# VectorE's scores on ScalarE's free rows, and packed Q and attention outputs, in a two-layer attention and mixer kernel

## The chip, the core and the metric

The kernel runs on one core of one Trainium2 chip. The metric is device time in microseconds. The program is one launch, with all inputs and the output in device memory.

## The reference

Two layers, each an attention block and a mixer block with an MLP, on one sequence of S = 2048 tokens of width D = 512, in bfloat16:

```
def A(x, wq, wk, wv, wo):              # 32 heads of width 16, one shared K and V
    q = heads(x @ wq); k = x @ wk; v = x @ wv
    p = softmax(einsum("bhqd,bkd->bhqk", q, k) * 16 ** -0.5)
    return merge(einsum("bhqk,bkd->bhqd", p, v)) @ wo
def B(x, w1, w2, w3, w4):
    h = gelu(layernorm(x) @ w1)
    hs = shift(h quarters by +1, -1, +2, -2 tokens) @ w2
    x1 = x + hs
    return x1 + gelu(layernorm(x1) @ w3) @ w4     # w3: 512 x 1792
for layer in range(2):
    x = x + A(layernorm(x), ...)
    x = x + B(layernorm(x), ...)
```

The scores are 32 x 2048 x 2048 per layer; their exponentials are most of the elementwise work.

## The kernel before

**The program is written by a planner.** `Plan` (line 32) is a small simulator that runs when the kernel is built. Each `op` has an engine, what it reads and writes, a guessed duration and a priority (a lower number goes first). `run` steps through time, `_pick` chooses for each free engine the ready operation of lowest priority number, `_place` gives it its start. `emit` then writes each engine's instructions in that fixed order, with semaphore waits. On the chip the order does not change. A DMA goes to SP's queue; each has a semaphore of its own.

**Attention.** A layer's queries are cut into chunks (`CHUNKS`, line 450): four of 512 tokens in layer 0; three of 512 and two of 256 in layer 1. Within a chunk, the loops run over 8 blocks `b` of four heads, over 16 key tiles `kb` of 128 tokens, and over two halves `p` of two heads each. A half is a unit: 2 heads x 128 keys x 512 queries (with 256 queries, two key tiles). There are 2048 units. The heads of a block lie in four groups of 32 SBUF rows, of which 16 carry data, so the score matmul of one head (`qk`, line 846) uses 32 of the array's 128 rows, and matmuls of different heads can run at the same time.

A unit goes one of two ways:
- `declare_unit` (line 879): two score matmuls into two PSUM banks (slots 0-1 and 2-3 in turn), one exponential of 128 x 1024 on ScalarE into EA (line 895), and the product with V (line 966), which adds into the bank ACC.
- `declare_pair` (line 901): two score matmuls (line 851) into two banks of the common pool, two VectorE instructions that write the exponent bits as uint16 into J (line 916), two shift adds of 43 and 85 into JK (line 924), and three products with V copies scaled by `PARTS`. So a pair is two L916, two L924 and three times the V product.

`assign` (line 1063) decides which units become pairs. It looks `AHEAD` = 7 halves ahead for one whose half is `ndve % 2`, so pairs take the two halves in turn; at most two pairs are unfinished, and VectorE's backlog must be under 4 us. It is called whenever the planner's time moves on (`pump`, line 1038). A pair's scores have priority 0.5, but `deferred` (line 225) gives them `ALONE` = 11 except where they can join score matmuls that are just running: then, on other rows, they go beside them (riding).

The pool has three PSUM banks (5, 6, 7), shared by pairs and by all side work.

**Side work.** `block_end` (line 974) closes a block: a copy of ACC (L998), sums, reciprocals, a product that spreads them (L1020), and a multiplication into OT (L1026). After a chunk's last block, `chunk_end` (line 1086) declares the output projection (L1124: eight matmuls of 16 used rows in 32 per tile, WO being padded with zeros), the mixer, the MLP, in layer 0 the next layer's layer norm, K and V, and the Q projection of the chunk after next (`qproj`, line 765). The Q projection writes each block with four column groups of 32, so that head h lands on rows 32h (L781, 16 matmuls a block), and one copy (L788). Side work has priority 10, behind the V products (2) and ahead of lone pairs; `URGE` sets a chunk's own number (1.5 for layer 0's last chunk), and `PACE` spreads its PE work. The mixer's Y tiles are a ring of six, so a chunk's mixer waits for the MLP of the tiles that hold its slots.

In layer 1, chunk 0 begins before all keys are there (`EARLY`); its partial sums are copied out (`SPILL`), and the Q of chunk 1 is written as they come free.

**Dummy matmuls.** `filler` (L868) puts a 512-column matmul of zeros on PE when the planner's running account (`KEEP`, `CREDIT`, `CAP`, `URGENT`, `FORCE`) finds that PE has worked too little. Side matmuls of full width are taken in its place where some are ready.

**Engines.** ScalarE has the exponentials and the GELUs, VectorE the pairs, all copies out of PSUM and the layer norms' elementwise work, POOL the roots of the variances and fills, SP the loads and 16 output stores.

Of the kernel before, what the change touches and what calls it, by code (L numbers as in the profile page):

```python
# [26 lines left out]
class Op:  # L27
    __slots__ = ("eng", "emit", "preds", "npend", "succ", "dur", "prio", "seq", "ready", "start",
                 "end", "take", "give", "dma", "out", "pos", "sem", "vc", "side", "placed", "pe", "feeds")


class Plan:
# [7 lines left out]
    DRAIN = {"ACT": 0.15, "DVE": 0.085, "POOL": 0.1}  # L40
    SELF = 0.035
    MARGIN = 0.2
# [5 lines left out]
    CREDIT = 0.3  # L48
    URGENT = 0.4
    FORCE = 0.6  # L50
    CAP = 1.0
    WAITING = 12.0
    BUNCH = 2
    ALONE = 11
    PATIENCE = 3.0
    SLACK = 0
    NEAR_FILL = 0.2

    def __init__(self, nc, pool_banks):
# [14 lines left out]
        self.lane = [0.0] * 4  # L74
        self.window = 0
# [8 lines left out]
        self.units = []  # L84

    def op(self, eng, emit, reads=(), writes=(), dur=0.1, prio=None, take=None, give=None,
           dma=0, out=False, side=True, pe=None):
# [3 lines left out]
        o.pe = pe  # L91
        o.feeds = None
# [184 lines left out]
    def _place(self, o, t):  # L277
# [5 lines left out]
        if o.dma:  # L283
            s = max(t + 1.6, self.dma_free)
            o.end = s + o.dma / 330e3 + 0.6
            self.dma_free = s + o.dma / 330e3
            self.free_at[o.eng] = t + 0.06
# [21 lines left out]
        else:  # L309
            self.free_at[o.eng] = t + o.dur  # L310
            o.end = t + o.dur + self.DRAIN[o.eng]
        heapq.heappush(self.events, self.free_at[o.eng])
        if o.give is not None:
            self.pool.append((o.end, o.give.bank))
            self.pool_last[o.give.bank] = o
            heapq.heappush(self.events, o.end + self.LAT["PE"])
            heapq.heappush(self.events, o.end + self.MARGIN)
        for s in o.succ:
# [42 lines left out]
    def emit(self):  # L361
# [6 lines left out]
        nd = 0  # L368
        for o in todo:
            kn = known[o.eng]  # L370
            cand = []
# [19 lines left out]
            if o.dma:  # L391
                nd += 1
                key = f"d{nd}"
                sems[key] = nc.alloc_semaphore(key)
                o.sem = (key, 16)
# [13 lines left out]
        def body(eng):  # L409
            def f(e):  # L410
                for waits, emit, sem, inc in code[eng]:
                    for k, v in waits:
                        e.wait_ge(sems[k], v)
                    emit(e).then_inc(sem, inc)
# [33 lines left out]
class Kernel:  # L448
# [4 lines left out]
    URGE = ((10, 10, 10, 1.5), (10, 10, 10, 10, 10))  # L453
# [8 lines left out]
    STEPS = (0, 43, 85)  # L462
    PARTS = (0.3203125, 0.25390625, 0.2021484375)
# [3 lines left out]
    AHEAD = 7  # L467
    MAX_PAIRS = 2
    BACKLOG = 4
# [24 lines left out]
    def memory(self):  # L494
# [13 lines left out]
        self.WO = sb("WO", [8, 512])  # L508
# [8 lines left out]
        self.OT = sb("OT", [8, 512])  # L517
# [14 lines left out]
        self.SM = sb("SM", [5, 16], dt.float32)  # L532
# [34 lines left out]
    def build(self):  # L567
        with contextlib.ExitStack() as self.stack:
# [3 lines left out]
            self.pl.filler = self.filler if self.FILL else None  # L572
            self.pl.run(self.pump)
            self.pl.emit()

    def head(self):
# [42 lines left out]
        for j in range(3):  # L619
            fill("POOL", self.VD[:, j, :, :, 16:17], self.PARTS[j], vd, 0.2, -7)  # L620
        for c in range(4):
# [3 lines left out]
            if c == 0:  # L625
                self.qproj(0, 0, prio=-6, blocks=(0,))
            if c == 2:
                self.qproj(0, 0, prio=-5, blocks=range(1, 8))
# [5 lines left out]
        fill("POOL", self.WO, 0.0, [("WO",)], 3.5, 3)  # L634
        fill("POOL", self.GP[:, 0, :, 0:2], 0.0, [("GPL", 0)], 0.1, 3)
        wo4 = ins["A_wo"].rearrange("(b g d) n -> g d b n", b=8, g=4, d=16)
        for g in range(4):
            load(self.WO[32 * g:32 * g + 16, :, :], wo4[g], [("WO",)], 131072, 5)
# [15 lines left out]
    def rstd(self, tiles, prio, both=False):  # L654
# [4 lines left out]
        s0, s1, s2, s3, s4 = (self.SM[:, i, a:b] for i in range(5))  # L659
# [10 lines left out]
        root(s0, mv, s4, tg("MV"), tg("R1"), tg("S4"))  # L670
        if both:
# [4 lines left out]
            root(s3, s2, s4, tg("S2"), tg("R2"), tg("S4"))  # L676

# [24 lines left out]
    def ln_in(self, la, tiles, prio=None):  # L702
# [6 lines left out]
        for tb in tiles:  # L709
            op("DVE", lambda e, tb=tb: e.tensor_scalar(  # L710
                out=self.ZR[:, tb % 4, :], in0=src(tb), scalar1=self.MV[:, tb, 0:1],
                scalar2=self.SM[:, 0, tb:tb + 1], op0=ALU.subtract, op1=ALU.mult),
               reads=[("X", tb), ("MV", tb), ("R1", tb)], writes=[("ZR", tb % 4)], dur=0.456 if la else 0.355, prio=prio)
# [51 lines left out]
    def qproj(self, la, c, prio=None, blocks=range(8)):  # L765
# [7 lines left out]
        for b in blocks:  # L773
# [18 lines left out]
    def make_groups(self):  # L792
# [34 lines left out]
        self.di = 0  # L827
# [10 lines left out]
        self.pairs = []  # L838
# [480 lines left out]
```

## Time and profile before

| | us |
|---|---|
| median of 3 runs (1708.56 to 1714.65) | 1708.66 |
| the profiled execution | 1708.95 |
| its span, first to last instruction | 1707.2 |
| PE busy, matmul | 1672.0 |
| ScalarE busy | 1545.6 |
| VectorE busy | 1398.7 |
| POOL busy | 62.6 |
| mean granted TensorE clock, share | 0.999 |

A row of a group reads: line, engine, operation, output and inputs with their shapes, count | busy time, mean ns of one | idle time of the engine just before them, and what ended it. A row of the waits reads: who waited for whom, us in total, times, longest. Times of stretches count from the span's start. PE's busy time has overlapping matmuls and modelled ends, so a busy PE is not PE at its peak.

### The profile page before, as it was taken

How to read it: one execution, taken by the hardware profiler on the slowest of the kernel's cores; microseconds unless marked ns; L12 is line 12 of the kernel's file. 1: busy time of each engine (PE TensorE's matmuls, PEld its weight loads, DVE VectorE, ACT ScalarE, POOL GpSimd, SP SyncE). 2: the span in 40 equal slices, each digit the busy share in tenths (PEclk: the TensorE clock that was granted, in tenths of full speed). 3: DMA queues.
4: the chain of work that ended last, by engine and by line, in shares of the span. 5: the costliest groups of instructions: out<-in, count | busy, mean ns of one | idle time of the engine just before them, and what ended most of it. 6: DMA issues, size and time to landing. Idle time of an engine off the chain costs nothing.

```text
span 1707.2 us, 37918 instructions
## 1 busy us (share of the span) xinstructions
PE 1672.0 (98%) x16522; PEld 555.0 (33%) x16522; DVE 1398.7 (82%) x2957; ACT 1545.6 (91%) x1632; POOL 62.6 (4%) x129
## 2 busy tenths in 40 slices
PE   8999999999999999999999999999999999999999
PEld 3322223323322222323223432223223224444444
DVE  8887999889998789898677568899889988668752
ACT  3999999999999999998978499999999999998912
POOL 2000000000000000000000000000000000000000
PEclk9999999999999999999999999999999999999999
DMA  5000000000000000000000000000000000000000
GB/s 186 2 1 1 1 1 1 1 1 1 2 2 1 1 1 1 2 1 1 1 1 1 1 1 2 2 1 2 5 4 4 2 1 2 8 8 2 2 13 16
DMA packets 10199, 12.42 MB, mean 7 GB/s; under 512 B 1584, under 2 KB 9520, under 8 KB 10032
## 3 DMA queue, kind: packets, MB, share of 16 engines
q1 hardware_dynamic: 10032, 10.00, 1.8%
q8 instruction: 129, 2.11, 0.5%
q14 instruction: 38, 0.31, 0.1%
HBM read 7.90 MB, written 2.10 MB: 6 GB/s over the span
## 4 chain that ended last, share of the span: by engine, by line
ACT 52%; PE 43%; DVE 4%; DMA 0%; issue 0%; POOL 0%; SPq 0%; POOLq 0%
ACT EA L895 48%; PE PB L851 14%; PE PB L966 11%; PE PB L1267 4%; PE PB L1236 4%; PE PB L868 3%; ACT G L1253 2%; PE PB L1124 2%; PE PB L1203 1%; PE PB L781 1%; ACT L895 1%; DVE J L916 1%; PE PB L690 1%; PE PB L1159 1%; DVE ST L649 1%; PE PB L1020 1%
## 5 line engine op out<-in xcount | busy, mean ns | idle before, releaser
L895 ACT ACTIVATE EA<-PB 128x1024 bf16<-128x1024 f32 x1558 | 1438.7, 1077 | 93.0 <-PE PB L851 56.6
L916 DVE TENSOR_SCALAR J<-PB 128x512 uint16<-128x512 f32 x980 | 634.4, 684 | 100.5 <-PE PB L851 95.5
L851 PE MATMUL PB<-QT,KT 32*128 32x512 bf16 (+1 forms) x4608 | 661.9, 359 | 14.4 <-ACT EA L895 9.9
L966 PE MATMUL PB<-EA,VP 128*32 128x512 bf16 (+1 forms) x3510 | 416.6, 360 | 1.0 <-DVE ACCF L994 0.3
L924 DVE TENSOR_SCALAR JK<-J 128x1024 uint16<-128x1024 uint16 x980 | 363.4, 420 | 37.7 <-PE PB L966 35.5
L851 PEld LDWEIGHTS PB<-QT,KT 32*128 32x128 bf16 x4608 | 172.2, 91 | 553.9 <-ACT EA L895 431.1
L966 PE MATMUL PB<-JK,VD 128*32 128x512 bf16 (+1 forms) x2196 | 256.9, 361 | 0.3 <-DVE JK L924 0.3
L966 PE MATMUL PB<-J,VD 128*32 128x512 bf16 (+1 forms) x1098 | 158.9, 362 | 0.4 <-DVE J L916 0.2
L966 PEld LDWEIGHTS PB<-EA,VP 128*32 128x32 bf16 x3510 | 111.7, 94 | 129.6 <-issue 107.2
L868 PE MATMUL PB<-ONES,NIL 128*128 128x512 bf16 x421 | 135.8, 394 | 11.5 <-DVE ST L649 2.5
L1236 PE MATMUL PB<-ZT,W 128*128 128x384 bf16 (+2 forms) x560 | 125.4, 339 | 0.4 <-DVE X L1130 0.3
L1267 PE MATMUL PB<-W,G 128*128 128x512 bf16 x448 | 121.4, 382 | 1.7 <-ACT G L1253 1.5
L966 PEld LDWEIGHTS PB<-JK,VD 128*32 128x32 bf16 x2196 | 71.4, 95 | 91.2 <-issue 47.9
L1246 DVE CAST G<-PB 128x512 bf16<-128x512 f32 (+2 forms) x126 | 73.2, 583 | 21.1 <-PE PB L1236 18.7
L781 PE MATMUL PB<-YT,WQ 128*32 128x512 bf16 (+1 forms) x1152 | 77.0, 359 | 0.1
L1124 PE MATMUL PB<-WO,OT 128*128 128x512 bf16 x256 | 74.1, 383 | 0.0
L868 PEld LDWEIGHTS PB<-ONES,NIL 128*128 128x128 bf16 x421 | 36.1, 98 | 86.6 <-issue 23.3
L1253 ACT ACTIVATE G<-G 128x3584 bf16<-128x3584 bf16 (+2 forms) x18 | 46.0, 2601 | 18.2 <-DVE G L1246 18.1
L666 POOL TENSOR_SCALAR SM<-MV 128x4 f32<-128x4 f32 (+3 forms) x30 | 8.9, 295 | 1363.7 <-DVE MV L651 1363.7
L1236 PEld LDWEIGHTS PB<-ZT,W 128*128 128x128 bf16 x560 | 41.4, 97 | 48.9 <-issue 26.3
L1026 DVE TENSOR_TENSOR OT<-ACCF,PB 128x512 bf16<-128x512 bf16 (+1 forms) x72 | 44.7, 622 | 11.6 <-PE PB L1020 11.2
L966 PEld LDWEIGHTS PB<-J,VD 128*32 128x32 bf16 x1098 | 43.2, 94 | 30.3 <-issue 22.2
(83 smaller groups left out, 850.2 us busy)
## 6 DMA issues: line engine op xcount, KB each, us to landing
W<-in_B_w_dram SPq DMA_DIRECT2D x2, 1792.0 KB, 12.3
X<-in_A_x_dram SPq DMA_DIRECT2D x8, 256.0 KB, 6.4
out_dram<-OUTB SPq DMA_DIRECT2D x16, 128.0 KB, 1.7
W<-in_B_w_dram SPq DMA_DIRECT2D x2, 512.0 KB, 6.5
WQ<-in_A_wq_dram SPq DMA_DIRECT2D x1, 512.0 KB, 5.8
WO<-in_A_wo_dram SPq DMA_DIRECT2D x4, 128.0 KB, 3.2
WK<-in_A_wk_dram SPq DMA_DIRECT2D x1, 16.0 KB, 6.0
WV<-in_A_wv_dram SPq DMA_DIRECT2D x1, 16.0 KB, 6.0
```

Source lines behind the costliest of these rows:

```text
L781: ins = e.matmul(self.PB[32 * g:32 * g + 32, L.bank, 0:n], lhsT=self.WQ[:, dc, w0:w0 + 32], rhs=self.YT[:, slot, dc, n0:n0 + n], start=(dc ...
L851: ins = e.matmul(self.PB[:, bank, j * n:(j + 1) * n], lhsT=self.KT[32 * h:32 * h + 32, la, (kb + j) * 128:(kb + j + 1) * 128], rhs=self.QT ...
L868: "PE", lambda e: e.matmul(self.PB[:, self.ACC if L is None else L.bank, :], lhsT=self.NIL, rhs=self.ONES, start=L is not None, stop=L is ...
L895: o = q.feeds = op("ACT", lambda e: e.activation(self.EA[:, ea, :, :], self.PB[:, b0:b0 + 2, :], ACTF.Exp, scale=0.25), writes=bk + [("EA" ...
L916: o = op("DVE", lambda e, i=i, L=L: e.tensor_scalar(out=J[:, i * 512:(i + 1) * 512], in0=self.PB[:, L.bank, :], scalar1=128 * LOG2E * 0.25 ...
L924: o = op("DVE", lambda e, k=k, r=r: e.tensor_scalar(out=self.JK[:, r, :], in0=J, scalar1=float(self.STEPS[k]), scalar2=None, op0=ALU.add), ...
L966: ins = e.matmul(self.PB[32 * h:32 * h + 32, self.ACC, 0:w], lhsT=v[:, la, kb + j, :], rhs=ap[:, i, j * w:(j + 1) * w], start=first and j ...
L1124: ins = e.matmul(self.PB[:, L.bank, :], lhsT=self.OT[:, b, q:q + 128], rhs=self.WO[:, b, :], start=(b == 0), stop=(b == 7))
L1236: ins = e.matmul(self.PB[:, L.bank, 0:n], lhsT=self.W3[:, dc, f * 128:(f + 1) * 128], rhs=ZT[:, dc, 0:n], start=(dc == 0), stop=(dc == 3))
L1246: op("DVE", lambda e, f=f, L=L: e.tensor_copy(self.G2[:, f, 0:n], self.PB[:, L.bank, 0:n]), writes=[L, ("G2", f)], dur=t_ps(n), give=L)
L1253: ins = e.activation(self.G2[:, a:a + 7, 0:n], self.G2[:, a:a + 7, 0:n], ACTF.Gelu_apprx_tanh)
L1267: ins = e.matmul(self.PB[:, L.bank, :], lhsT=self.G2[:, f, i * 128:(i + 1) * 128], rhs=self.W4[:, f, :], start=(f == 0), stop=False)
```

## The change

**Riding by rule.** When the planner places a score matmul of a ScalarE unit, it now calls `attach`: if two pool banks are free, a pair of the other half is declared at once. `assign` takes the half as an argument, looks between 2 and 22 halves ahead, and is otherwise called only when no pair was declared for 4 us.

```
+        if o.feeds is not None and self.attach is not None:
+            self.attach(o)
...
-        if self.assign(now):
+        if now > self.attached + self.LONELY and self.assign(now, self.ndve % 2):
...
+    def attach(self, q):
+        if sum(1 for t, b in self.pl.pool if t + 0.06 <= self.pl.now) >= self.FREE:
+            self.assign(self.pl.now, 1 - q.pe[3][0] // 2)
...
-        d = max(self.di, self.hi + self.AHEAD)
-        while d < len(self.halves) and (self.halves[d][7] or self.halves[d][5] != self.ndve % 2):
+        d = self.hi + self.AHEAD
+        while d < len(self.halves) and (self.halves[d][7] or self.halves[d][5] != p or d in self.given):
             d += 1
-        if d >= len(self.halves):
+        if d >= min(len(self.halves), self.hi + self.AHEAD + self.FAR):
             return False
```

**Constants.**

```
-    URGE = ((10, 10, 10, 1.5), (10, 10, 10, 10, 10))
+    URGE = ((10, 10, 10, 1.0), (10, 10, 10, 1.5, 10))
-    AHEAD = 7
+    AHEAD = 2
-    BACKLOG = 4
+    BACKLOG = 6
+    FAR = 20
+    FREE = 2
+    LONELY = 4
-    MARGIN = 0.2
+    MARGIN = 0.15
-    CREDIT = 0.3
-    URGENT = 0.4
+    CREDIT = 0.2
+    URGENT = 0.6
-    CAP = 1.0
-    WAITING = 12.0
+    CAP = 0.5
+    WAITING = 16.0
-    ALONE = 11
+    ALONE = 8
-    SLACK = 0
+    SLACK = 0.05
```

**Q packed.** Except for blocks 0 and 1 of the first chunk and all of layer 1's chunk 1 (`direct`), Q is projected two blocks at a time with all 128 columns (4 matmuls for each two blocks), copied to QS, and moved to the rows 32h of QT by two operations of four DMAs each. QT is cleared once by POOL.

```
+        for k in () if direct else range(blocks[0] // 2, blocks[-1] // 2 + 1):
...
+                        ins = e.matmul(self.PB[:, L.bank, 0:n], lhsT=self.WQ[:, dc, 128 * k:128 * k + 128],
+                                       rhs=self.YT[:, slot, dc, n0:n0 + n], start=(dc == 0), stop=(dc == 3))
...
+            op("DVE", lambda e, k=k, L=L: e.tensor_copy(self.QS[:, k, 0:n], self.PB[:, L.bank, 0:n]),
...
+            for j in range(2):
+                op("SP", lambda e, j=j: [
+                    e.dma_start(self.QT[32 * h:32 * h + 16, par, 2 * k0 + j:2 * k1:2, 0:n],
+                                self.QS[64 * j + 16 * h:64 * j + 16 * h + 16, k0:k1, 0:n]) for h in range(4)],
```

**Attention outputs packed.** L1026 writes OS (two slots) in place of OT, and four DMAs move the 16 used rows of each head into an OT of four full tiles. WO is no longer padded (one load in place of four and a clearing), and the output projection takes 4 matmuls per tile.

```
+        op("SP", lambda e: [
+            e.dma_start(self.OT[r0 + 16 * h:r0 + 16 * h + 16, b // 2, 0:n], self.OS[32 * h:32 * h + 16, m, 0:n])
+            for h in range(4)], reads=[("OS", m)], writes=[("OT", b)], dma=128 * n, parts=4, prio=5)
...
-        for h in range(4):
+        for h in range(2):
...
-                                   start=(b == 0), stop=(b == 7))
+                                   start=(b == 0), stop=(b == 3))
```

An operation of the planner may now hold several DMAs (`parts`); the DMAs use 80 semaphores in turn, each waiting for the last use of its own.

**Shift adds.** A constant second operation is added; the code can put adds and layer-norm products on POOL, but `ADDS = 0` and `LN_ENG = "DVE"` keep them on VectorE.

```
-            o = op("DVE", lambda e, k=k, r=r: e.tensor_scalar(
-                out=self.JK[:, r, :], in0=J, scalar1=float(self.STEPS[k]), scalar2=None, op0=ALU.add),
+            x = op(eng, lambda e, k=k, r=r: e.tensor_scalar(
+                out=self.JK[:, r, :], in0=J, scalar1=float(self.STEPS[k]), scalar2=1.0, op0=ALU.add,
+                op1=ALU.mult),
```

The same second operation (`scalar2=0.0, op1=ALU.add`) stands in the product L1143.

149 lines of the change are left out of this document (101 added, 48 removed).

## The prediction

> **What bounds the kernel now.** I read the busy time by stage first (columns: stretch, its length, busy time and instructions of PE, PEld, DVE, ACT and POOL, granted clock, DMA share, GB/s), then the costliest groups, then the waits of each stage.
>
> ```profile
> 50.00:750.00 700.00, 694.89 (x6606) 206.47 (x6600) 620.16 (x1299) 695.91 (x741) 17.61 (x36) 1.00 0.01 1
> 750.00:1000.00 250.00, 239.03 (x1846) 80.39 (x1844) 176.77 (x372) 200.03 (x202) 10.45 (x20) 1.00 0.00 1
> 1000.00:1450.00 450.00, 446.63 (x4645) 138.21 (x4642) 394.55 (x822) 448.47 (x480) 9.18 (x19) 1.00 0.01 2
> 1450.00:1620.00 170.00, 165.39 (x2454) 71.24 (x2453) 130.09 (x289) 158.94 (x165) 7.85 (x16) 1.00 0.02 5
> 1620.00:1707.00 87.00, 81.23 (x450) 39.80 (x448) 35.37 (x75) 19.99 (x25) 4.98 (x14) 1.00 0.04 14
> ...
> 450.00:500.00 50.00, 49.61 (x492) 15.21 (x494) 47.91 (x99) 49.93 (x53) 0.19 (x1) 1.00 0.01 1
> ```
>
> In three stages (50 to 750, 1000 to 1450, 1450 to 1620) ScalarE is full or nearly so: 1303.3 of 1320 us. In the fourth, around the change of layer (750 to 1000), it is idle for 50 us, and in the tail the work is a chain with little in parallel. PE looks full everywhere, but that counts dummy matmuls and overlapping ends. VectorE is idle for 79.8 + 55.5 + 39.9 = 175.2 us in the three stages where ScalarE is the limit. So time can come from two places: units moved from ScalarE to VectorE, and an earlier end of the side work that stands alone at 750 to 1000 and after 1620.
>
> ```profile
> L895 ACT ACTIVATE EA<-PB 128x1024 bf16<-128x1024 f32 x1558 | 1438.7, 1077 | 93.0 <-PE PB L851 56.6 <-PE PB L966 35.4
> L916 DVE TENSOR_SCALAR J<-PB 128x512 uint16<-128x512 f32 x980 | 634.4, 684 | 100.5 <-PE PB L851 95.5
> L924 DVE TENSOR_SCALAR JK<-J 128x1024 uint16<-128x1024 uint16 x980 | 363.4, 420 | 37.7 <-PE PB L966 35.5
> ...
> L868 PE MATMUL PB<-ONES,NIL 128*128 128x512 bf16 x421 | 135.8, 394 | 11.5 <-DVE ST L649 2.5 <-DVE MV L651 1.7 <-DVE ZR L1222 1.6
> L781 PE MATMUL PB<-YT,WQ 128*32 128x512 bf16 (+1 forms) x1152 | 77.0, 359 | 0.1
> L1124 PE MATMUL PB<-WO,OT 128*128 128x512 bf16 x256 | 74.1, 383 | 0.0
> ```
>
> There are 2048 units: 1558 exponentials on ScalarE at 1438.7/1558 = 0.923 us, and 490 pairs on VectorE (two L916, two L924 each) at (634.4 + 363.4)/490 = 2.036 us.
>
> **Riding.** The price of a pair's scores that do not ride stands in two bursts of L851 of four matmuls each, two for a ScalarE unit and two for a pair: where both use the same two heads they take 0.60 us, where they use different ones 0.39.
>
> ```profile
> 122.50 0.60 PE L851 MATMUL PB<-QT,KT 32*128 32x512 bf16 x4
> 126.05 0.39 PE L851 MATMUL PB<-QT,KT 32*128 32x512 bf16 x4
> ...
> 126.52 1.29 DVE L916 TENSOR_SCALAR J<-PB 128x512 uint16<-128x512 f32 x2 [1.21 <-PE PB L851]
> 127.72 1.42 DVE L924 TENSOR_SCALAR JK<-J 128x1024 uint16<-128x1024 uint16 x4
> 129.23 1.29 DVE L916 TENSOR_SCALAR J<-PB 128x512 uint16<-128x512 f32 x2
> ```
>
> Today the pair's heads alternate by count, so riding is luck; what does not ride waits at priority 11, behind all side work. The change declares a pair when a ScalarE unit is placed, for the other two heads, if two banks are free, and lowers the lone priority to 8. What that can give back is the time VectorE waits for L851 (first row of each stage; the second is the wait of L924 for a buffer that L966 still reads):
>
> ```profile
> DVE J L916 <- PE PB L851: 40.7, 57, 4.0
> DVE JK L924 <- PE PB L966: 15.4, 19, 2.0
> ...
> DVE J L916 <- PE PB L851: 18.3, 37, 1.6
> DVE JK L924 <- PE PB L966: 9.3, 21, 1.3
> ...
> DVE J L916 <- PE PB L851: 14.7, 16, 6.1
> DVE JK L924 <- PE PB L966: 5.9, 7, 1.6
> ```
>
> That is 73.7 us in the three stages. I take three quarters, 55 us; nothing of the 30.6 us on L966, since more pairs bring more of those matmuls.
>
> **Repacked Q.** Q blocks of 16 used rows in 32 become full 128-row products. Directly written stay 2 blocks of the first chunk and the 8 of layer 1's chunk 1; the rest become 3 + 5 x 4 copies of 512 columns and 8 of 256. So of 72 copies 31 go: 23 long ones and 8 short ones.
>
> ```profile
> L788 DVE CAST QT<-PB 128x512 bf16<-128x512 f32 x56 | 37.7, 684 | 5.0 <-PE PB L781 4.8
> L788 DVE CAST QT<-PB 128x256 bf16<-128x256 f32 x16 | 6.5, 413 | 1.1 <-PE PB L781 1.0
> ```
>
> 23 x 37.7/56 + 8 x 6.5/16 = 18.7 us of VectorE. With the 55 us that is 74 us. A pair moved costs VectorE 2.036 us and shortens the stage by 0.923, in which VectorE would also have worked, so 74/(2.036 + 0.923) = 25 pairs, and ScalarE's stages end 25 x 0.923 = **23 us earlier**. The planner's other constants (margins, credits, how far ahead a pair may lie) change only the order that it writes; no row prices them, and I leave them inside these bounds. With no wait gone, 18.7/2.96 = 6 pairs, 6 us; with VectorE as full as at 450 to 500 (47.91 of 50, so 55 us of idle left in 1320), (175 - 55 + 18.7)/2.96 = 47 pairs, 43 us. A loss is a rival below.
>
> **The shift add** gets a second operation (multiply by one). No row shows a constant second one. Two rows differ by an operation and a pointer:
>
> ```profile
> L1143 DVE TENSOR_SCALAR ZR<-Y,SM 128x512 bf16<-128x512 bf16 x32 | 10.5, 343 | 0.1
> L710 DVE TENSOR_SCALAR ZR<-X,MV,SM 128x512 bf16<-128x512 bf16 x16 | 5.8, 405 | 0.0
> ```
>
> At worst 62 ns on each of 980 adds, 61 us, 61/2.96 = 21 pairs, 19 us. I take zero: L916 already does two operations, and the pointer is the likelier owner of the 62 ns; the end stays in the range. The ZR product L1143 gets the same second operation, at worst 2 us in all. The POOL paths of the adds and layer norms are switched off and cost nothing.
>
> **PE slots and the tail.** A 512-column slot costs 3.02/14 = 0.216 us:
>
> ```profile
> 1632.59 3.02 PE PB L1267 x14
> ```
>
> Four 32-column L781 matmuls share a slot, so 72 blocks are 288 slots; after, 10 x 4 + 31 x 4 = 164. The 124 saved (92 long, 32 half as long) are 23 us. L1124 goes from 256 to 128 matmuls, 128 x 0.216 = 28 us. Of these 51 us, the layer-1 part ahead of the tail is chunk 2's Q (16 slots), chunks 3 and 4 (32 half slots) and 14 tiles of L1124 (56 slots): 104 - 16 = 88 slots, 19 us. In the tail the chain stands so:
>
> ```profile
> 1617.29 2.85 ACT L895 ACTIVATE EA<-PB 128x1024 bf16<-128x1024 f32 x3 [0.55 <-PE PB L966]
> 1624.43 6.27 ACT L1253 ACTIVATE G<-G 128x3584 bf16<-128x3584 bf16 x2 [2.99 <-DVE G L1246]
> 1635.87 0.69 DVE L1278 TENSOR_TENSOR OUTB<-PB,X 128x512 bf16<-128x512 f32 x1 [3.94 <-PE PB L1263]
> 1636.48 0.54 DVE L1139 TENSOR_SCALAR Y<-X,MV,SM 128x512 bf16<-128x512 f32 x1
> ```
>
> After the last exponential (1620.1) the MLP of chunk 2 is still to get its GELU, and chunk 3's mixer starts only at 1636.5, when that MLP has freed the ring of six Y tiles. Side work is last in priority, so 19 us of PE freed ahead of it pull this MLP forward, and chunk 3's own work now has urgency 1.5. I take 13 of the 19, since 170 us with PE at 165.4 also hold dummies that free slots may only replace. Chunk 4's chain gets new links: four DMAs after the last block, then 8 matmuls where 16 stood.
>
> ```profile
> L1282 SPq DMA_DIRECT2D out_dram<-OUTB x16: 332/332/372, 1230.4 to 1705.0; - x16
> out_dram<-OUTB SPq DMA_DIRECT2D x16, 128.0 KB, 1.7
> WK<-in_A_wk_dram SPq DMA_DIRECT2D x1, 16.0 KB, 6.0
> ```
>
> No copy inside the chip stands in the trace. Four issues and a landing lie between 4 x 0.33 + 1.7 = 3.0 us and 1.3 + 6.0 = 7.3; I take 3.0, because the 6.0 was taken behind the input loads, less 8 x 0.216 = 1.7 saved: +1. Tail: **-12 us**, bounds -30 (most of chunk 2's 26 us gone) and +6.
>
> SP's queue gets 64 Q issues and 288 for the outputs, 3 less for WO: 349 x 0.33 = 116 us over the span. SP has nothing but 16 output stores after the loads, which come behind them in the queue. A DMA that waits for VectorE holds those behind it; Q is double-buffered by chunk, so that costs nothing unless it is the last output of a chunk.
>
> **Change of layer and head.** The 50 us that ScalarE is idle at 750 to 1000 are a chain of GELUs, layer norms and W4 products. 16 of its slots go (3.5 us), urgency rises from 1.5 to 1.0, and a DMA wait of 3.0 us (which the next chunk's units can cover) comes in. I take **-5**, bounds -15 and +8. In the head, 12 slots (2.6 us) and three copies (2.0) go: **-2**, bounds -4 and +2; the new clearing of QT takes about the place in which POOL clears WO today.
>
> The sum: -23 - 12 - 5 - 2 = -42. The profiled execution took 1708.95 us (span 1707.2), against a median of 1708.66, so no correction: **1667 us**.
>
> **Rivals.** *VectorE is its own limit.* The waits for L851 close, but the time goes to waits for L966 and for side work's banks, and the freed slots are filled with dummies. Then 6 us from the copies and some 5 from tail and head remain: 1698. For it: POOL and banks are unchanged, and L924's 30.6 us are there already. Against: at 126 to 130 L916, L924 and L916 follow each other with no gap once scores are early. The Trainium skill, "TensorEngine Tiling (Array Packing)", section PSUM Bottleneck, says that packing speeds up TensorE but not the emptying of PSUM, which may become the bound; by that alone this rival would hold. The trace agrees in part: the pair above needs 1.29 us to empty what PE wrote in 0.39.
>
> *Fewer pairs (slower).* A pair needs two of three banks free at the moment a unit's scores are placed; where side work holds two, the fallback gives one pair per 4 us. L916 ran 488 times in 50 to 750, a pair per 2.87 us:
>
> ```profile
> 50.00:750.00 700.00, 315.24 (x488) 1.00 0.01 1
> ```
>
> If half of the 1320 us fell to one per 4 us, 660 x (1/2.87 - 1/4) = 65 pairs went back to ScalarE, +60 us, less 19 of the other terms: 1750. It decides once more than 19/0.923 = 21 pairs are lost. For it: side work is in most stretches. Against: a pair's banks are empty 1.29 us after its scores, and units come every 0.92.
>
> *The clock.* In the head, a stretch with PE busy 1.71 of 3.4 us was followed by one at a granted 0.53, with 8 matmuls in 3.11 us.
>
> ```profile
> 5.40:8.80 3.40, 1.71 (x7) 1.00 1.02 334
> 8.80:12.20 3.40, 3.11 (x8) 0.53 1.10 309
> ```
>
> Such a stretch loses 3.11 - 8 x 0.216 = 1.4 us of PE. With 51 us of dense work out and dummies rarer (cap 0.5, urgent 0.6), 40 of them would cost 56 us of PE, of which I let half reach the end: 1667 + 28 = 1695. Against: every stage after the head was granted 1.00. [...]
>
> *More.* VectorE as full as at 450 to 500 and chunk 2's MLP out of the tail: 1708.95 - 43 - 30 - 5 - 2 = 1629.
>
> *Not done.* If the planner finds no free banks at all, every pair comes from the fallback, which is the slower rival at its end and counted in it.
>
> **How the numbers follow.** Forecast 0.56, VectorE its own limit 0.15, fewer pairs 0.12, clock 0.05, more 0.12. The forecast's own range is 1640 to 1700. For 8 in 10 the range runs from 1624 (just past "more") to 1712 (past the limit and clock rivals, and 1667 with the add's 19 us and the upper ends of tail and change of layer, 18 + 13, which is 1717, all but reached); fewer pairs and a remainder are left out. A measurement tells about 0.5%, 8.5 us: faster is under 1700.1, slower over 1717.2. Faster: 0.54 + 0.12 + 0.07 of the limit and clock rivals = 0.73; slower: most of fewer pairs and the add's worst end, 0.12; same 0.15.
>
> **What would show it.** Right: some 1030 L916 and 1533 exponentials; VectorE's wait for L851 under 25 us in the three stages; bursts of four at 0.39 us; 284 Q and 128 output matmuls; the add still at 420 ns; 75 us from last exponential to end; SP issues landing within about 2 us. Wrong: fewer than 980 L916, an add of 480 ns, stages with a clock under 1.00, dummies well above 421, or a tail still of 87 us.

## The result, and the profile after

The changed kernel takes **1650.28 us** (median of 4 runs, 1650.17 to 1650.58), beside 1709.0 for the kernel before (4 runs, 1708.56 to 1714.65): a ratio of 0.9649, 95% interval 0.9629 to 0.967. The forecast was 1667, with a range of 1624 to 1712. The profiled execution has a span of 1648.8 us, 58.4 less than before.

Lines have moved: the exponential is now L961, the scores L917, the V product L1039, the exponent bits L982, the shift add L992, the dummies L934. The first view is the busy time by stage (columns as in the prediction):

```profile
50.00:750.00 700.00, 681.48 (x6193) 206.16 (x6271) 626.31 (x1307) 698.09 (x743) 18.28 (x36) 1.00 0.04 7
750.00:1000.00 250.00, 238.01 (x2049) 81.17 (x2078) 204.20 (x442) 219.04 (x224) 11.06 (x20) 1.00 0.01 3
1000.00:1450.00 450.00, 438.07 (x4404) 140.14 (x4442) 398.53 (x828) 445.42 (x471) 13.67 (x25) 1.00 0.04 9
1450.00:1620.00 170.00, 162.73 (x2156) 74.20 (x2174) 134.09 (x295) 140.84 (x143) 8.61 (x22) 1.00 0.03 9
1620.00:1648.00 28.00, 24.76 (x130) 11.86 (x131) 6.22 (x15) 6.88 (x14) 1.11 (x2) 1.00 0.04 15
```

ScalarE is as full as before from 50 to 750 and from 1000 to 1450. Around the change of layer it now works 219.04 of 250 us where it worked 200.03, and the granted clock is 1.00 in every stage. The costliest groups, of the kernel after:

```profile
L961 ACT ACTIVATE EA<-PB 128x1024 bf16<-128x1024 f32 x1541 | 1425.2, 1058 | 57.1 <-PE PB L1039 31.5 <-PE PB L917 24.3
L982 DVE TENSOR_SCALAR J<-PB 128x512 uint16<-128x512 f32 x1014 | 656.4, 683 | 103.9 <-PE PB L917 100.0
L992 DVE TENSOR_SCALAR JK<-J 128x1024 uint16<-128x1024 uint16 x1014 | 381.8, 419 | 21.3 <-PE PB L1039 15.7
L934 PEld LDWEIGHTS PB<-ONES,NIL 128*128 128x128 bf16 x340 | 28.7, 98 | 71.8 <-issue 27.9 <-DVE J L982 12.4 <-DVE JK L992 5.2
L828 DVE CAST QS<-PB 128x512 bf16<-128x512 f32 (+1 forms) x31 | 18.7, 609 | 1.5 <-PE PB L824 1.3
```

There are 17 units fewer on ScalarE (1558 to 1541) and 17 pairs more (980 to 1014 L982). The add with two operations costs 419 ns, as with one. Dummies fell from 421 to 340; they are counted by their weight loads here, because some matmul records are missing (276 of 340 are there).

The end of the span, in ScalarE's timeline of the kernel after (start, length, what it did, what it was idle for before):

```profile
1546.92 6.27 ACT L1330 ACTIVATE G<-G 128x3584 bf16<-128x3584 bf16 x2
...
1575.42 1.06 ACT L1253 ACTIVATE GP<-GP 128x1024 bf16<-128x1024 bf16 x1
1586.26 1.02 ACT L961 ACTIVATE EA<-PB 128x1024 bf16<-128x1024 f32 x1 [0.50 <-PE PB L917]
1600.79 3.28 ACT L1330 ACTIVATE G<-G 128x1792 bf16<-128x1792 bf16 x2 [12.21 <-DVE G L1323]
```

In the kernel before, chunk 2's MLP GELU (the 128 x 3584 one) ran at 1624.43, behind the last exponential, and chunk 3's mixer GELU later still:

```profile
1648.23 1.06 ACT L1173 ACTIVATE GP<-GP 128x1024 bf16<-128x1024 bf16 x1 [17.53 <-DVE GP L1169]
```

Now the MLP GELU starts 39 us before the last exponential does, and chunk 3's mixer GELU is ahead of it too. What is left behind the last exponential is chunk 3's MLP and chunk 4.

A span can be added up along ScalarE: its idle time in the first 50 us, its busy time up to the last exponential, its idle time around the change of layer (750 to 1000 us), its other idle time before the last exponential, and the tail behind that. From the two traces, in us:

| | before | after | difference |
|---|---|---|---|
| idle, head | 27.7 | 22.6 | -5.1 |
| busy up to the last exponential | 1525.8 | 1524.7 | -1.1 |
| idle, change of layer | 50.0 | 31.0 | -19.0 |
| other idle | 16.7 | 9.0 | -7.7 |
| tail | 87.0 | 61.5 | -25.5 |
| span | 1707.2 | 1648.8 | -58.4 |

The busy time hides two movements: exponentials fell by 13.5 us (1438.7 to 1425.2), and some 12 us of GELUs and table loads came in: 7 of them stood in the tail before, and four more table loads (34 for 30, 1.28 us each) make 5. Three quarters of the gain (19.0 and 25.5) lie where side work stands alone.

### The profile page after: what moved, and what is told of

It is laid out like the page before. It is cut to its first block, busy times and chain, and to the rows that moved or that the text cites. A ratio compares the mean times of both kernels' runs of the same rounds, so it can differ in the third digit from the quotient of the medians.

```text
span 1648.8 us, 36207 instructions
## 1 busy us (share of the span) xinstructions
PE 1589.5 (96%) x15333; PEld 531.6 (32%) x15521; DVE 1413.3 (86%) x2994; ACT 1537.7 (93%) x1619; POOL 67.9 (4%) x130
## 4 chain that ended last, share of the span: by engine, by line
ACT 60%; PE 35%; DVE 3%; issue 1%; DMA 0%; POOL 0%; SPq 0%; POOLq 0%
ACT EA L961 56%; PE PB L917 11%; PE PB L1039 9%; PE PB L1344 5%; PE PB L1313 3%; ACT G L1330 2%; PE PB L1206 1%; PE PB L1239 1%; ACT L961 1%; PE PB L737 1%; DVE J L982 1%; PE PB L934 1%; PE PB L824 1%; ACT GP L1253 1%; DVE ST L677 1%
## 5 line engine op out<-in xcount | busy, mean ns | idle before, releaser
L961 ACT ACTIVATE EA<-PB 128x1024 bf16<-128x1024 f32 x1541 | 1425.2, 1058 | 57.1 <-PE PB L1039 31.5
L982 DVE TENSOR_SCALAR J<-PB 128x512 uint16<-128x512 f32 x1014 | 656.4, 683 | 103.9 <-PE PB L917 100.0
L917 PE MATMUL PB<-QT,KT 32*128 32x512 bf16 (+1 forms) x4608 | 624.7, 360 | 20.9 <-ACT EA L961 15.4
L1039 PE MATMUL PB<-EA,VP 128*32 128x512 bf16 (+1 forms) x3472 | 450.8, 361 | 1.7 <-DVE ACCF L1067 0.5
L992 DVE TENSOR_SCALAR JK<-J 128x1024 uint16<-128x1024 uint16 x1014 | 381.8, 419 | 21.3 <-PE PB L1039 15.7
L917 PEld LDWEIGHTS PB<-QT,KT 32*128 32x128 bf16 x4608 | 159.1, 91 | 540.8 <-ACT EA L961 462.3
L1039 PE MATMUL PB<-JK,VD 128*32 128x512 bf16 (+1 forms) x2272 | 316.4, 360 | 0.9 <-DVE JK L992 0.7
L1039 PE MATMUL PB<-J,VD 128*32 128x512 bf16 (+1 forms) x1136 | 182.5, 361 | 4.1 <-DVE J L982 4.1
L1039 PEld LDWEIGHTS PB<-EA,VP 128*32 128x32 bf16 x3472 | 118.8, 94 | 142.6 <-issue 122.0
L1039 PEld LDWEIGHTS PB<-JK,VD 128*32 128x32 bf16 x2272 | 88.6, 95 | 98.0 <-issue 49.8
L934 PE MATMUL PB<-ONES,NIL 128*128 128x512 bf16 x276 | 90.2, 395 | 7.9 <-DVE ZR L720 2.2
L1330 ACT ACTIVATE G<-G 128x3584 bf16<-128x3584 bf16 (+2 forms) x18 | 46.0, 2601 | 16.4 <-DVE G L1323 16.3
L1039 PEld LDWEIGHTS PB<-J,VD 128*32 128x32 bf16 x1136 | 49.0, 94 | 37.1 <-issue 23.7
L1099 DVE TENSOR_TENSOR OS<-ACCF,PB 128x512 bf16<-128x512 bf16 (+1 forms) x72 | 44.7, 620 | 10.3 <-PE PB L1093 8.0
L934 PEld LDWEIGHTS PB<-ONES,NIL 128*128 128x128 bf16 x340 | 28.7, 98 | 71.8 <-issue 27.9
L1344 PEld LDWEIGHTS PB<-W,G 128*128 128x128 bf16 x448 | 31.3, 97 | 49.5 <-issue 30.4
L677 DVE BATCH_NORM_STATS2 ST<-X 128x6 f32<-128x512 f32 (+1 forms) x64 | 42.9, 678 | 3.7 <-DMA X<-in_A_x_dram 3.3
```

The lines of the kernel that those rows point to most:

```text
L677: op("DVE", lambda e, tb=tb: e.bn_stats(self.ST6[:, tb, :], src(tb)), reads=[tagf(tb)], writes=[("ST", tb)], dur=0.606, prio=prio)
L917: ins = e.matmul(self.PB[:, bank, j * n:(j + 1) * n], lhsT=self.KT[32 * h:32 * h + 32, la, (kb + j) * 128:(kb + j + 1) * 128], rhs=self.QT ...
L934: "PE", lambda e: e.matmul(self.PB[:, self.ACC if L is None else L.bank, :], lhsT=self.NIL, rhs=self.ONES, start=L is not None, stop=L is ...
L961: o = q.feeds = op("ACT", lambda e: e.activation(self.EA[:, ea, :, :], self.PB[:, b0:b0 + 2, :], ACTF.Exp, scale=0.25), writes=bk + [("EA" ...
L982: o = op("DVE", lambda e, i=i, L=L: e.tensor_scalar(out=J[:, i * 512:(i + 1) * 512], in0=self.PB[:, L.bank, :], scalar1=128 * LOG2E * 0.25 ...
L992: x = op(eng, lambda e, k=k, r=r: e.tensor_scalar(out=self.JK[:, r, :], in0=J, scalar1=float(self.STEPS[k]), scalar2=1.0, op0=ALU.add, op1 ...
```

## The experiments

The prediction's theory: freed PE slots end side work sooner, and VectorE's freed time takes pairs from ScalarE at 0.923 us a unit, so the parts add. The rivals: VectorE is its own limit, so that little but the copies counts; the clock, because dummies are made rarer; and, formed on the result, that no part brings much alone, because a freed slot that the planner fills with a dummy or leaves to work that isn't late is worth little: only the parts together bring the side work of a chunk ahead of the point where ScalarE runs out. Last, that one order of instructions is luckier than another.

The change has three parts, and each experiment takes the kernel after and undoes some:
- **packing** (Q and attention outputs): undone, `direct` is always true, the outputs go straight into the padded OT, and WO is padded;
- **riding**: undone, `attach` isn't set, `assign` is the old one, with `AHEAD = 7`, `BACKLOG = 4`, `ALONE = 11`;
- **constants**: undone, `DRAIN`, `MARGIN`, `CREDIT`, `URGENT`, `CAP`, `WAITING`, `SLACK` and `URGE` are the old ones. `DRAIN` is the planner's guess of how long after an operation its result counts as ready; for POOL it went from 0.1 to 0.0, which the section on the change does not list.

The second operation of the adds and the planner's guesses for DMAs stay new in every run, and no run undoes all three parts at once.

All runs in one table. The kernel before, run beside them, had medians of 1712.67 (e1 to e4), 1709.38 (e5 to e8) and 1713.64 (e9 to e12); ratios are to it. The five parts of the span are those of the table above, taken from each run's profiled execution; "half clock" is its time granted 0.5, inside the span.

| run | median, us | ratio (95%) | pairs | head | busy | change of layer | other | tail | dummies | half clock |
|---|---|---|---|---|---|---|---|---|---|---|
| before | 1709.0 | 1 | 490 | 27.7 | 1525.8 | 50.0 | 16.7 | 87.0 | 421 | 3.4 |
| after | 1650.28 | 0.9649 (0.9629-0.967) | 507 | 22.6 | 1524.7 | 31.0 | 9.0 | 61.5 | 340 | 3.4 |
| e1 packing | 1693.89 | 0.9892 (0.9858-0.9925) | 503 | 22.2 | 1513.2 | 51.7 | 10.1 | 93.6 | 519 | 0 |
| e2 riding | 1706.85 | 0.998 (0.9957-1.0003) | 499 | 26.0 | 1528.6 | 53.8 | 16.3 | 80.2 | 360 | 3.4 |
| e3 constants | 1728.57 | 1.01 (1.0067-1.0132) | 494 | 25.8 | 1524.4 | 57.7 | 31.5 | 87.5 | 303 | 64.9 |
| e4 packing, riding | 1681.18 | 0.9816 (0.9783-0.9848) | 506 | 27.4 | 1520.4 | 38.0 | 15.9 | 79.1 | 430 | 20.5 |
| e5 all but urgencies | 1661.64 | 0.9723 (0.9708-0.9737) | 503 | 22.5 | 1525.4 | 28.6 | 7.2 | 75.9 | 379 | 3.4 |
| e6 urgencies, other constants old | 1673.07 | 0.9798 (0.9772-0.9825) | 510 | 27.4 | 1508.2 | 45.1 | 18.5 | 80.1 | 427 | 23.9 |
| e7 all but packing | 1697.73 | 0.9937 (0.992-0.9953) | 497 | 27.2 | 1532.4 | 50.8 | 14.9 | 70.6 | 305 | 10.2 |
| e8 all but riding | 1689.83 | 0.9884 (0.9869-0.9899) | 492 | 23.9 | 1525.7 | 41.1 | 19.5 | 79.0 | 372 | 41.0 |
| e9 more pairs | 1699.39 | 0.9924 (0.9898-0.9951) | 551 | 27.5 | 1470.9 | 89.1 | 16.4 | 93.8 | 333 | 51.2 |
| e10 adds on GpSimd | 1674.97 | 0.9762 (0.971-0.9813) | 503 | 21.5 | 1514.2 | 45.5 | 2.3 | 79.2 | 399 | 0 |
| e11 one guess changed | 1656.66 | 0.9667 (0.9629-0.9706) | 507 | 22.6 | 1519.9 | 37.7 | 7.5 | 67.3 | 363 | 3.4 |
| e12 eight EA buffers | 1639.57 | 0.9572 (0.9526-0.9618) | 502 | 22.2 | 1525.6 | 21.6 | 2.2 | 66.2 | 326 | 0 |

(The profiled execution of e6 took 1681.04, 8 us more than its median; that of e10 1664.42, 10.6 less, e10's executions reaching to 1679.21.) Where a run's gain or loss is given in microseconds below, it is its ratio taken of 1709.

Half clock has a price that the executions show. The four of e6 have spans of 1669.1 us (two of them, mean granted clock 1.000), 1673.4 (0.997) and 1679.2 (0.993). A mean of 0.993 is 2 x 0.007 x 1679.2 = 23.5 us at half clock, and they cost 10.1: 0.43 us for each. The kernel before, run beside e1 to e4, gives 0.42 (1705.8 at 1.000, 1718.8 at 0.991). At 0.43, as an estimate, the half clock beyond the 3.4 us that the kernels before and after have cost e3 some 26 us, e9 21, e8 16 and e4 7.

**e1, packing alone.** Riding and constants undone:

```
-            self.pl.attach = self.attach
...
-        if now > self.attached + self.LONELY and self.assign(now, self.ndve % 2):
+        if self.assign(now):
```

> The changed program with the old riding rule (halves in turn, AHEAD 7, BACKLOG 4, ALONE 11) and the old planner constants and urgencies: only Q and the attention outputs are packed. Theory A (PE slots freed by packing let the side work end earlier): most of the 58 us, 1665 to 1680, with the tail from last exponential to end near 65 us and about as many exponentials as before (1545 to 1565). Theory B (riding by rule is what counts): 1695 or more. Theory C (constants and urgencies): 1695 or more.

It gained 18 us (1693.89): against theory A, and just below the 1695 of B and C. There are 13 pairs more (503) and ScalarE is 12.6 us less busy, but the side work did not end sooner: change of layer 51.7, tail 93.6. Here are the dummies, and ScalarE's timeline at the end, of this kernel:

```profile
L934 PEld LDWEIGHTS PB<-ONES,NIL 128*128 128x128 bf16 x519 | 43.5, 97 | 100.7 <-issue 27.1 <-DVE J L982 16.8 <-DVE JK L992 10.4
```

```profile
1559.05 38.03 ACT L961 ACTIVATE EA<-PB 128x1024 bf16<-128x1024 f32 x41
1597.10 1.28 ACT L1331 ACT_TABLE_LOAD   x1
1608.20 6.27 ACT L1331 ACTIVATE G<-G 128x3584 bf16<-128x3584 bf16 x2 [9.82 <-DVE G L1324]
```

Of the 252 slots' worth of matmuls taken out (124 Q and 128 output), 98 stand there again as additional dummies, and chunk 2's MLP GELU still stands behind the last exponential, 11 us behind it where it was 4 before.

**e2, riding alone.** Packing and constants undone:

```
+        direct = True
...
-                                   start=(b == 0), stop=(b == 3))
+                                   start=(b == 0), stop=(b == 7))
```

> The changed program with Q and outputs unpacked as before and the old constants: only the riding rule (with its AHEAD, BACKLOG, FAR, FREE, LONELY, ALONE). Theory A: a small gain, 1690 to 1705, PE still late, tail near 87 us. Theory B: 1665 to 1680, with 1535 to 1545 exponentials. Theory C: no change within 8 us.

1706.85, ratio 0.998 (0.9957 to 1.0003), as in theory C: nothing that can be told from no change, though the bursts of four score matmuls (four that start within 0.06 us) rose from 215 to 424. PE is busy for 1638.3 us in place of 1672.0, with 61 dummies fewer, and the span is 2.3 us shorter: the PE time that riding frees by itself goes unused.

**e3, constants alone.** Packing and riding undone; the constants are the new ones.

```
-            self.pl.attach = self.attach
+        direct = True
```

> The changed program with unpacked Q and outputs and the old riding rule: only the planner's constants (margin, credit, cap, urgent, waiting, slack, drain) and the urgencies of layer 0's last chunk and layer 1's fourth. Theories A and B: within 10 us of 1709. Theory C: 1665 to 1680, with the idle time of ScalarE around the change of layer down from 50 to about 31 us.

1728.57, 17 us slower than before, and outside the ranges of all three theories. The stages of this kernel show it (the column before the last two is the granted clock):

```profile
750.00:1000.00 250.00, 234.80 (x1744) 79.70 (x1763) 175.32 (x373) 192.34 (x194) 9.60 (x20) 0.97 0.00 1
1000.00:1450.00 450.00, 429.82 (x4231) 132.48 (x4271) 378.22 (x788) 431.96 (x460) 9.28 (x19) 0.95 0.01 2
```

The clock rival is real here: with 303 dummies in place of 421, 64.9 us ran at half clock, 47.8 of them from 933 to 1066, in and behind the change of layer. ScalarE's idle time grew by 7.7 us at the change of layer and by 14.8 elsewhere. The spans differ by 19.7 us (1726.9 and 1707.2), of which half clock takes some 26 by the price above: without it the constants alone would have gained about 7 (an estimate).

**e4, packing and riding.** Old constants only:

```
-    CAP = 0.5
+    CAP = 1.0
```

(and the other constants likewise)

> Packing and riding together, old constants and urgencies. Theory A: 1650 to 1665, packing alone less another 10 to 15. Theory B: near riding alone, 1660 to 1675. Theory C: 1690 or more, since what is missing is the cause.

1681.18, between the ranges of the theories: a gain of 31 where e1 and e2 add up to 22. The constants, worth -17 alone, are worth 29 on top of these two, some 7 of them (by the price of half clock) because e4 has 20.5 us at half clock.

**e5, the old urgencies.**

```
-    URGE = ((10, 10, 10, 1.0), (10, 10, 10, 1.5, 10))
+    URGE = ((10, 10, 10, 1.5), (10, 10, 10, 10, 10))
```

> The changed program with the two urgencies as before (layer 0's last chunk 1.5, layer 1's fourth chunk 10). So far packing alone gave 1694, packing and riding 1681, all together 1650. Theory D (freed PE slots shorten the layer change and the tail only where side work is put ahead): 1675 to 1685, tail 75 to 80 us. Theory E (the dummies' rules: with the old ones dummies take the freed slots): 1650 to 1660, tail near 62 us, dummies near 341.

1661.64, 13 us of the gain lost. The tail has it: 75.9 for 61.5, with the other four parts within 2.5 us of the kernel after. The tail is the one that theory D gave, the time is nearer to E's. ScalarE's timeline of this kernel:

```profile
1567.79 6.27 ACT L1330 ACTIVATE G<-G 128x3584 bf16<-128x3584 bf16 x2
...
1599.05 1.06 ACT L1253 ACTIVATE GP<-GP 128x1024 bf16<-128x1024 bf16 x1 [14.02 <-DVE GP L1249]
1616.88 3.28 ACT L1330 ACTIVATE G<-G 128x1792 bf16<-128x1792 bf16 x2 [16.78 <-DVE G L1323]
```

The last exponential ends at 1583.7 here. Chunk 2's MLP is ahead of it without any urgency, but chunk 3's mixer GELU is not: ScalarE waits 14.02 us for it.

**e6, the new urgencies with the old dummy rules.** e4 with the new `URGE`.

```
-    URGENT = 0.6
+    URGENT = 0.4
```

(with `DRAIN`, `MARGIN`, `CREDIT`, `CAP`, `WAITING` and `SLACK` old as well)

> Packing, riding and the two new urgencies, with the margins and the rules of the dummies as before. Theory D: 1650 to 1662, tail near 62 us and layer change near 31 us although dummies stay near 430. Theory E: 1675 to 1685.

1673.07, just under theory E's range: the urgencies bring 3 us on top of e4, against 13 on top of e5. With 427 dummies the change of layer stays at 45.1 and the tail at 80.1, in an execution with 23.9 us at half clock.

**e7, all but packing**, and **e8, all but riding.**

```
e7:
+        direct = True
e8:
-            self.pl.attach = self.attach
```

> The changed program with Q and the outputs unpacked as before, all else kept. Theory A in its joint form (packing frees the slots that the other parts use): 1690 to 1712, so that packing is worth 40 to 60 us on top of the others against 18 alone. Theory that the parts add up (packing 18, riding 4 to 13, the rest 31): 1665 to 1672.

> The changed program with the old riding rule, all else kept. If riding only adds (its 13 us on top of packing): 1663. If riding is needed for the others (lone scores hold PE where dummies are rarer): 1680 to 1700. VectorE's wait for scores should be near the 95 to 100 us that both kernels show, in either case.

1697.73 and 1689.83, both in the ranges of the joint forms: on top of the others packing is worth 49 us and riding 40, where alone they were worth 18 and 3. Packing's 49 lie at the change of layer (50.8 to 31.0), the tail (70.6 to 61.5), ScalarE's busy time, idle time and head. Without riding the rare dummies again leave 41.0 us at half clock, which makes some 16 of riding's 40 (by the price above); with riding and packing together the same rules leave 3.4. VectorE's wait for scores was 117.1 us in e8, not 95 to 100.

**e9, more pairs.** A lone pair is declared after 2 us without one, not 4:

```
-    LONELY = 4
+    LONELY = 2
```

> The changed program with LONELY 2 in place of 4: 551 pairs and 1497 exponentials are written in place of 507 and 1541. Theory F (the prediction's term: a pair moved ends ScalarE's stages 0.923 us earlier, VectorE has the time): 1612 to 1630. Theory G (what VectorE has left belongs to the side work's copies; more pairs hold banks and PE and push the side work back): 1665 to 1690, with a layer change and tail as long as before.

This falls against the term by which I had priced the steady stages, and lies above theory G's range too. With 44 more pairs the exponentials fell by 41.4 us (1425.2 to 1383.8), another 12 us of GELUs and table loads are no longer ahead of the last exponential (7 stand behind it, 5 are four table loads fewer), and the kernel took 47 us more than after. Its stages:

```profile
50.00:750.00 700.00, 679.80 (x6178) 198.10 (x6244) 645.00 (x1360) 689.85 (x736) 15.14 (x29) 0.98 0.03 7
750.00:1000.00 250.00, 231.46 (x1693) 84.70 (x1712) 188.16 (x409) 160.92 (x158) 12.87 (x27) 0.96 0.02 3
```

VectorE is fuller (645.00 for 626.31), and ScalarE stands idle 89.1 of the 250 us around the change of layer, the tail is 93.8, and the clock fell to half for 51.2 us, some 21 of the 47. The lone pairs don't ride (203 bursts of four and 293 of one, against 445 and 70 in the kernel after). That PE so loses slots which the side work wanted, and that ScalarE waits for it, is argued; no run shows it apart from the clock.

**e10, up to two shift adds in flight on GpSimd.**

```
-    ADDS = 0
+    ADDS = 2
```

> The changed program with up to two shift adds at a time on GpSimd. If GpSimd's adds take VectorE's 0.38 us each away from it and nothing else: 1635 to 1650. If they are slow (the planner assumes 1.12 us) and hold the J buffers longer, or slow VectorE's own work: 1655 to 1690, with VectorE's add longer than 0.42 us where both run.

1674.97, 19 us of the gain lost. The groups of the add in this kernel, first GpSimd's, then VectorE's:

```profile
L992 POOL TENSOR_SCALAR JK<-J 128x1024 uint16<-128x1024 uint16 x649 | 707.7, 1090 | 733.8 <-DVE J L982 511.6 <-PE PB L1039 154.3 <-DVE MV L679 24.3
L982 DVE TENSOR_SCALAR J<-PB 128x512 uint16<-128x512 f32 x1006 | 649.8, 683 | 182.4 <-PE PB L917 176.2
L992 DVE TENSOR_SCALAR JK<-J 128x1024 uint16<-128x1024 uint16 x357 | 216.5, 621 | 11.2 <-PE PB L1039 7.1
```

GpSimd takes 649 adds, which would have cost VectorE 272 us; but the 357 that stay cost 621 ns, not 419, and what VectorE does gain goes into waiting for scores (176.2 for 100.0). VectorE is 123 us less busy (1289.9 for 1413.3), and there are 503 pairs, four fewer than in the kernel after: less work on VectorE brought no pair. The planner's rules set the number of pairs, so this does not show what limits them.

**e11, one guess changed.** A guess of the planner by which only the order can move:

```
-    DRAIN = {"ACT": 0.15, "DVE": 0.085, "POOL": 0.0}
+    DRAIN = {"ACT": 0.15, "DVE": 0.085, "POOL": 0.1}
```

> The changed program with one guess of the planner put back: 0.1 us after a GpSimd operation. No instruction is added or removed by it but what the planner's choices bring; it measures how far an accidental change of order moves the time. If orders are worth little: 1647 to 1653. If the order is a lucky one among many: 1655 to 1675, and differences of that size between the other runs prove little.

1656.66, in the range of the lucky order: 3 us slower by the ratios and 6.1 by the spans, with the same 507 pairs: change of layer +6.7, tail +5.8, busy -4.8. So an order has some 6 us of luck in it, by this one trial, and I make little of differences under 10 us between two plans. The 13 of the urgencies and the 13 of e12 are near that; the 29, 40 and 49 of the three parts are not.

**e12, eight EA buffers.** ScalarE's wait for L1039 is the V product that must have read a buffer of EA before the exponential writes it:

```
-    N_EA = 7
+    N_EA = 8
```

> The changed program with eight EA buffers in place of seven. ScalarE waits 31.5 us for V products that still read EA (PE L1039). If that wait is of buffers: 1632 to 1645. If it is the layer change's own lateness: within 6 us of 1650.

1639.57, in the range for a wait of buffers, and the fastest kernel here: 0.9572 (0.9526 to 0.9618), below the interval of the kernel after. By the spans it is 11.1 us faster than the kernel after. The waits of ScalarE in it:

```profile
ACT EA L961 <- PE PB L917: 26.7, 17, 17.8
...
ACT EA L961 <- PE PB L1039: 12.7, 7, 6.7
```

The wait for L1039 fell from 31.5 to 12.7 us, change of layer and other idle by 9.4 and 6.8; the tail gave 4.7 back.

## Why the prediction was right, and where its terms were not

**Direction and mechanism.** The kernel got faster by what was named: side work that ends sooner at the change of layer and ahead of the tail. ScalarE's last exponential ends at 1587.3, 32.8 us sooner than 1620.1; the terms for steady stages, change of layer and head made 30 of it. But that agreement, and that the time lies in the range, are in part luck. In the table above the steady stages (busy and other idle) gave 8.8 us, 14 less than forecast, while tail, change of layer and head gave 49.6, 31 more than their 19.

**Steady pairs, -23: mis-sized.** 17 pairs moved, not 25, so exponentials fell by 13.5 us. The copies' share was right: 31 of 72 went, and the 41 that stand (31 of QS at 18.7 us, 10 direct at 6.7) take 25.4 us, 18.8 less than the 44.2 before. The step that failed is "What that can give back is the time VectorE waits for L851 ... I take three quarters, 55 us". Here is that wait in the three stages, after (the first stage, then 1000 to 1450, then 1450 to 1620):

```profile
DVE J L982 <- PE PB L917: 45.5, 73, 2.1
DVE JK L992 <- PE PB L1039: 6.6, 10, 1.3
...
DVE J L982 <- PE PB L917: 27.8, 44, 2.2
DVE JK L992 <- PE PB L1039: 4.4, 8, 0.9
...
DVE J L982 <- PE PB L917: 12.2, 15, 1.8
DVE JK L992 <- PE PB L1039: 1.4, 4, 0.5
```

It is 85.5 us, where it was 73.7 and I had said under 25. It changed its kind: in the whole span there are more and shorter waits, the longest 2.2 us where it was 9.1. What VectorE waits for in them stays open. That it is the time until the rule declares the next pair would fit e9, where pairs that need not ride cut it to 68.5, but not e8, where the old rule declares them at any time and the wait is 117.1. The wait for L1039, of which I had counted nothing, fell from 30.6 to 12.4 instead. The rows of the whole span, before and after:

```profile
DVE J L916 <- PE PB L851: 95.5, 123, 9.1
...
DVE J L982 <- PE PB L917: 100.0, 153, 2.2
```

**Riding did happen.** PE's timeline of the kernel after, around 480 us, shows four matmuls in the time of two:

```profile
480.12 0.40 PE L917 MATMUL PB<-QT,KT 32*128 32x512 bf16 x4
481.10 0.39 PE L917 MATMUL PB<-QT,KT 32*128 32x512 bf16 x2 [0.26 <-ACT EA L961]
```

Bursts of four rose from 215 to 445, those of one and three fell from 608 to 164. What came of it is 206 PE bursts fewer, not time of VectorE. I had given riding no PE term.

**Packing.** Weight loads count the matmuls: 124 packed and 160 direct for Q, 128 for the outputs, as forecast.

```profile
L824 PEld LDWEIGHTS PB<-YT,WQ 128*128 128x128 bf16 x124 | 8.0, 97 | 12.8 <-issue 8.1 <-DVE JK L992 1.6 <-DVE J L982 0.9
L1206 PEld LDWEIGHTS PB<-WO,OT 128*128 128x128 bf16 x128 | 7.7, 97 | 14.2 <-issue 9.4 <-DVE J L982 2.0 <-DVE JK L992 1.6
L846 PEld LDWEIGHTS PB<-YT,WQ 128*32 128x32 bf16 x160 | 2.7, 95 | 3.7 <-issue 2.0 <-DVE KT L786 0.4 <-DVE JK L992 0.2
```

**Tail, -12: it was -25.5.** The step named the mechanism (chunk 2's MLP pulled ahead of the last exponential) and took 13 of 19 us, since the stretch also holds "dummies that free slots may only replace". That doubt was right for packing alone (e1) and wrong with the new constants: half of the tail's gain is gone without the urgencies (e5), and with the old dummy rules they don't bring it (e6). The links that the DMAs put into chunk 4's chain are longer than the 3.0 us taken. Rows of the two issuing lines (ns, shortest, median, longest) and of their landings, of the kernel after:

```profile
L1104 SPq DMA_DIRECT2D OT<-OS x288: 507/589/1768, 57.7 to 1593.6; - x144
...
DMA to landing us min/median/max: 1.6/1.8/4.0
```

```profile
OT<-OS SPq DMA_DIRECT2D x224, 16.0 KB, 1.8
QT<-QS SPq DMA_DIRECT2D x40, 64.0 KB, 2.4
```

An issue takes 0.59 us, not the 0.33 of an output store, so four and a landing are 4 x 0.59 + 1.8 = 4.2 us, and SP's new work is some 208 us (352 x 0.59), not 116. But no wait of PE, VectorE or ScalarE for one of these copies shows. The last four are issued from 1591.77 to 1594.17, and the product that reads them (L1206) starts at 1600.35, right behind chunk 3's MLP products on PE. So the links were covered and cost nothing that shows.

**Change of layer, -5: it was -19.0,** past my bound of -15. I had priced 16 slots by themselves; the runs show that no part alone shortens this stage (51.7, 53.8 and 57.7 us in e1, e2, e3), that packing does with riding (38.0, e4) or with the constants (41.1, e8), that riding with the constants but without packing doesn't (50.8, e7), and that all three do most. Which of the constants does it stays open: beside `URGE`, whose effect there is small, they were not tried one by one.

**Head, -2: -5.1.** Where packing stands with the old constants and riding (e4, e6) it isn't there, in e1 and e5 it is; that is left open.

**The add's second operation, 0: right** (419 ns).

**The rivals.** *VectorE is its own limit* gave 1698 from the copies and little else. Packing alone came out near it (1693.89) with other parts (busy time -12.6, head -5.5, tail +6.6), and e10 shows VectorE's time given away without a pair gained, but the whole change went past it. The Trainium skill, "TensorEngine Tiling (Array Packing)", section PSUM Bottleneck, says that the emptying of PSUM may become the bound. The trace does not decide that for the pairs, of which there are only 17 more; most of this change's gain (44.5 of 58.4 us) came from side work that ends sooner. *Fewer pairs* did not occur. *The clock* did not in the kernel after (3.4 us at half clock, all in the head), and did where the rare dummies stood without riding (e3, e8) or beside lone pairs (e9). Beside riding without packing (e7) 10.2 us ran at half clock. In number the dummies of e12 (326) are fewer than those of e8 (372), so their count alone does not decide it. *More* (1629) had nearly the tail (-30), but 43 us in the steady stages, which did not come.

So the cause that the runs bear out is the one formed afterwards: the parts are worth 18, 3 and -17 us one at a time, which makes 4, and 60 together. Of the 56 us between, half clock takes somewhat less than half (the 26 us that e3 loses to it, an estimate); the rest they bring only together. That a freed slot is worth what the rule that fills it makes of it fits the dummies of e1 and e6 and the unused PE time of e2, but it is argued from them.

## What to carry to other kernels

Price a freed slot by what will be put into it: if a planner or a dummy rule fills it, the slot may be worth little until that rule is changed with it, so test parts both alone and by leaving each out of the whole. An engine's waiting time isn't time to be had until it is known what it waits for: VectorE's wait for scores stayed although more scores rode, and its cause is still open. When dummies are made rarer, read the granted clock of every variant: here half clock alone made up much of what looked like one part needing another. When the busiest engine is full, look at the two places where it is idle; there one buffer more (e12) brought as much as the pairs moved.

## What the runs showed of the hardware

- **Half clock comes in blocks, behind a stretch with gaps.** In e3, e8 and e9 every stretch granted 0.5 between head and tail is 3.4 us long or a multiple of it (6.8, 10.2, 13.7, 27.3), as in the head. In all traces of this case each began behind 3.4 us in which PE was recorded busy for some 0.7 to 2.8 us (a few matmul records are missing). That is not enough for it to happen: in e10 PE was busy for 1.51 and 1.63 us in two stretches of 3.4 from 919.1 on, and the clock stayed at 1.00. An example from e3:

```profile
929.50:932.90 3.40, 1.23 (x7) 0.38 (x7) 0.00 (x0) 3.39 (x5) 0.00 (x0) 1.00 0.00 0
932.90:943.10 10.20, 10.16 (x35) 2.56 (x35) 1.29 (x2) 5.53 (x6) 0.00 (x0) 0.50 0.01 2
```

- **GpSimd's work slows VectorE's add.** Beside GpSimd's adds of the same shape (1090 ns), VectorE's went from 419 to 621 ns, while L982, which reads PSUM, stayed at 683. In e10 the 93 adds of VectorE that ran at no time beside one of GpSimd's took 416 ns, the other 264 took 692. The Trainium skill, "GPSIMD Engine Reference", section 1. Specifications, says that GpSimd shares its SBUF interfaces with VectorE, with contention for some kinds of VectorE instructions; the trace agrees for this add, and gives the size.
- **Copies between partitions land soon.** In the kernel after 16 KB land in 1.8 us and 64 KB in 2.4 (medians), but each issue holds its queue for 0.59 us.
